# Seven block products for half of B's query and key projections, with B's V of those tokens moved ahead of the rest

## The chip, the cores and the metric

One core of a Trainium2 chip runs the whole program. The metric is the device time of one execution in microseconds; the kernel before takes 1763.98 us (median of 3 runs, 1763.06 to 1763.99).

The core has a matrix engine (TensorE, PE in the profile, with its weight loads as PEld), a vector engine (DVE), a scalar engine (ACT), a general engine (POOL, GpSimd) and a queue that starts transfers (SP). Matmul results stand in eight banks of PSUM, each 128 rows of 512 numbers.

## The reference

Two attention blocks on 2048 tokens of 640 numbers, each with 32 heads of 20, and their results side by side:

```python
qkv = x @ wqkv                        # A and B: 2048 x 1920
# A: each query sees 8 keys, at distances 0, 2, ..., 14 behind it
logits = einsum("bhsd,bhswd->bhsw", q, kg) * Dh ** -0.5     # masked, softmax over 8
# B: full attention
scores = einsum("bhqd,bhkd->bhqk", q, k) * Dh ** -0.5       # softmax over 2048 keys
out = concatenate([A(o) @ wo, B(o) @ wo], axis=-1)
```

## The kernel before, in words

Every product of two fp32 matrices is made of three matmul passes: each operand is cast to a rounded high part on ACT, the low part (value minus high part) is made by a subtract on DVE, and PE adds high x high, high x low and low x high (PASSES, line 30: pairs of weight part and x part). A projection of one tile therefore takes 5 row parts of 128 (KC) x 3 passes = 15 matmuls.

The program is written out in one order. `pe`, `act`, `dve`, `gp` and `sp` (class InOrder, line 49) pin each instruction behind the one written before it on the same engine, so an engine never passes a waiting instruction; between engines only data and buffers order the work. Since all of them record through line 61, the profile shows this line for everything, and one reads it by tiles. `after(n, fn)` (line 80) puts work off to the n-th `tick()` from now; the main loops call `tick` once per group of matmuls, so work put off lands at a fixed group.

The stages, in the order of PE's queue:

1. A's projections (lines 524 to 578): four weight column groups n, twelve token tiles t of 128 each, 15 matmuls per tile, each result copied by ACT (`a_store`) and stored to DRAM. The other four token tiles of A are done later, in the loop. At tile 5 of each group `a_keep` copies the split weights to DRAM (`wa_d`, eight transfers) for them. During the last group B's inputs are loaded and split (`x_pieces`, `m_pieces`: DMA to a staging tile, cast on ACT, subtract on DVE).
2. B's q and k (lines 615 to 655): five pairs of weight blocks m (128 columns each, order MS: the five blocks of k, then of q) x four token blocks n of 512 x two blocks j, 40 groups of 15 matmuls of 128x512. The result is cast by ACT (`pr`), its low part made by DVE from PSUM, and both are stored to DRAM (`qb_d`, `kb_d`). Banks come from a rotation over all eight. The next pair's weights are loaded at n = 1 and split two ticks later.
3. B's V (lines 1026 to 1063): 30 groups (`v_group`) of 15 matmuls of 128x320, for token blocks 2, 3, 0, 1 and two halves of the columns; the last two groups (LAG) run inside the loop. ACT copies each into one of four tiles `ve` whose extra columns of ones were set at the start by POOL (`ones`). From the seventh group on each is followed by one step of maxima, `b_max`: four matmuls of q against k in two pairs of banks (`wide()`, two such pairs, banks 4 to 7) and two reduces on DVE, which give the running maximum of each query row; 24 steps (LEAD) are needed before the loop. Since x tiles 0 and 1 gave their place to q and k of attention, they are loaded and split a second time (groups 8 and 16).
4. The loop (from line 1094): scores, exponentials, the product with V and the rest of the maxima in a written order (UNIT, UNIT_V, ...), with A's remaining work between, and at the end both output projections.

A's own attention is POOL's work: `a_attention` (line 450) is a generator of pieces, each a handful of elementwise instructions on tile `akv`, whose data was fetched by SP two pieces before. `next(a_work)` writes one piece; twelve are written among the 40 groups of q and k and eight among the V groups. B's keys and queries for the loop (tiles `bk`, `bq`) are loaded by `b_keys` and `b_queries` in the last q and k groups and the first V groups.

Of the kernel before, what the change touches and what calls it, by code (L numbers as in the profile page):

```python
# [21 lines left out]
KC = 5  # L22
# [16 lines left out]
PB = 6  # L39
# [26 lines left out]
def attention_pair(ctx, tc, xa, wqk_a, wv_a, wo_a, xb, wqk_b, wv_b, wo_b, oa, ob):  # L66
# [270 lines left out]
    ones = [sb.tile([128, 16 * VC + 11], F32, tag=tag, bufs=2, name="ve") for tag in ("raw", "rb", "raw", "rb")]  # L337
    for t in ones:
        gp.memset(t, 1.0)
# [182 lines left out]
    MS = [5, 6, 7, 8, 9, 0, 1, 2, 3, 4]  # L522
    XB, WB = [], []
# [17 lines left out]
    for n in range(NA):  # L541
        nxt = None
        for t in range(UP):
# [20 lines left out]
            if n == 1 and t == 7:  # L564
                w, more = x_pieces(xb, 0)
                XB.append(w)
                loads += more
            if n == NA - 1:
                if t in (1, 2):
                    w, more = m_pieces(MS[t - 1])  # L570
                    WB.append(w)
                    more[0]()
                if t % 4 == 0 and t:
                    w, more = x_pieces(xb, t // 4)
                    XB.append(w)
                if t > 4 and t % 4:
                    more.pop(0)()
        W = nxt
    wait[0] = 2
    w, loads = x_pieces(xb, 3)  # L580
    XB.append(w)
# [34 lines left out]
    for m in range(0, 10, 2):  # L616
        nxt = []
        for n in range(4):
            for j in range(2):
                p = next(banks)  # L620
                for k in range(KC):
                    for i, (wi, xi) in enumerate(PASSES):
                        pe.matmul(p, WB[j][:, wi, k], chunk(XB[n], xi, k), start=(k == 0 and i == 0),
                                  stop=(k == KC - 1 and i == 2))
                c = MS[m + j]
                o = (0, 1) if c < KC else (1, 0)
                pt = sb.tile([128, 2, 512], F32R, tag="p", bufs=PB, name="pr")
                act.copy(pt[:, o[0]], p)
                dve.tensor_tensor(pt[:, o[1]], p, pt[:, o[0]].bitcast(F32), ALU.subtract)
                after(1, sp.dma_start, dst_b(c, n).rearrange("t p c -> p t c"), pt.bitcast(F32))  # L630
                tick()
                if loads:
                    loads.pop(0)()
                if m < 8 and (n, j) in ((1, 0), (1, 1)):
                    w, loads = m_pieces(MS[m + 2 + len(nxt)])
                    nxt.append(w)
                elif m == 8 and (n, j) == (0, 1):
                    WV, loads = wide_pieces(wv_b[0])
                elif m == 8 and n == 3:
                    if j == 0:  # L640
                        wait[0] = 4
                        w1, more = wide_pieces(wv_b[1])
                        for fn in more:
                            fn()
                if m == 8 and n > 1:
                    if (n, j) == (2, 0):
                        k_loads = b_keys(0)
                        rings.append(big(1, [128, NQC, 2, 512], "bq"))
                        q_loads = [fn for qc in range(NQC) for fn in b_queries(0, qc)]
                    k_loads.pop(0)()  # L650
                groups += 1
                if 4 < groups < 34 and groups * 2 % 5 < 2:
                    next(a_work, None)
        WB = nxt
    tick()

    def max_rows(m4, m1, q, qc):

        mt = sb.tile([128, 3, 32], F32R, tag="mtr", bufs=2, name="mtr")
# [366 lines left out]
    for n, half, s in V_GROUPS[:-LAG]:  # L1028
# [6 lines left out]
        if groups == 1:  # L1035
            wait[0] = 5
# [155 lines left out]
```

## Time and profile before

| | |
|---|---|
| time, median of 3 runs | 1763.98 us (1763.06 to 1763.99) |
| profiled execution: span from the first to the last instruction | 1761.2 us |
| granted clock of TensorE, mean | 1.000 |
| A's projections | 0 to 161.6 us |
| B's q and k | 161.6 to 300.5 us |
| B's V with 24 steps of maxima | 300.5 to 389.4 us |
| the loop and the end | 389.4 to 1761.2 us |
| busy: PE, DVE, ACT, POOL | 1749.3, 1345.8, 1333.5, 1229.1 us |

The profiled execution has no time of its own beside its span; the median lies 2.8 us above that span, and that difference (start and end of the execution around the first and the last instruction) is taken as the same for both kernels. A row of the timeline reads: start, duration, engine, line, operation, tile written <- tile read, shapes, count, and in brackets the idle time before it with what ended it. A row of the stretches reads: from:to, length, busy time of PE, weight loads, DVE, ACT and POOL with instruction counts, granted clock, share of the DMA engines, GB/s. PE's busy time holds the modelled ends of pipelined matmuls, so the distance between starts is what a matmul costs.

### The profile page before, as it was taken

How to read it: one execution, taken by the hardware profiler on the slowest of the kernel's cores; microseconds unless marked ns; L12 is line 12 of the kernel's file. 1: busy time of each engine (PE TensorE's matmuls, PEld its weight loads, DVE VectorE, ACT ScalarE, POOL GpSimd, SP SyncE). 2: the span in 40 equal slices, each digit the busy share in tenths (PEclk: the TensorE clock that was granted, in tenths of full speed). 3: DMA queues.
4: the chain of work that ended last, by engine and by line, in shares of the span. 5: the costliest groups of instructions: out<-in, count | busy, mean ns of one | idle time of the engine just before them, and what ended most of it. 6: DMA issues, size and time to landing. Idle time of an engine off the chain costs nothing.

```text
span 1761.2 us, 31938 instructions
## 1 busy us (share of the span) xinstructions
PE 1749.3 (99%) x11331; PEld 997.6 (57%) x11331; DVE 1345.8 (76%) x1821; ACT 1333.5 (76%) x2598; POOL 1229.1 (70%) x1086
## 2 busy tenths in 40 slices
PE   9999999999999999999999999999999999999999
PEld 8988888874444444444444444444444444444569
DVE  3102333679999999999999999999999999999400
ACT  4323222229989999999999999999999999989881
POOL 0000683595888888888989898988888898745442
PEclk9999999999999999999999999999999999999999
DMA  7657867774536554644474456536552634222223
GB/s 261 196 170 246 303 236 265 240 234 118 160 98 172 145 161 127 160 131 133 157 178 129 135 150 156 161 103 172 148 154 91 158 100 138 62 73 63 60 71 112
DMA packets 215176, 269.74 MB, mean 153 GB/s; under 512 B 91724, under 2 KB 131788, under 8 KB 215016
## 3 DMA queue, kind: packets, MB, share of 16 engines
q1 hardware_dynamic: 214440, 267.04, 51.3%
q8 instruction: 89, 1.46, 0.4%
q14 instruction: 71, 0.58, 0.1%
q10 hardware_dynamic: 576, 0.66, 0.1%
HBM read 192.87 MB, written 74.74 MB: 152 GB/s over the span
## 4 chain that ended last, share of the span: by engine, by line
PE 95%; DVE 2%; ACT 1%; DMA 1%; issue 1%; POOL 0%; SPq 0%; DVEq 0%; POOLq 0%; ACTq 0%
PE ps_st L61 95%; DVE mx L61 1%; ACT e L61 1%; DMA bq<-qb_d 1%; DMA stg<-wv_b 0%; ACT more L61 0%; DVE mtr L61 0%; SPq L61 0%; POOL am L61 0%; ACT al L61 0%; ACT pr L61 0%; DVE ww L61 0%; POOL ident L61 0%; ACT ro L61 0%; DVE am L61 0%
## 5 line engine op out<-in xcount | busy, mean ns | idle before, releaser
L61 DVE TENSOR_REDUCE mx<-ps_st 128x1 f32<-128x512 f32 (+1 forms) x1500 | 1217.4, 877 | 75.5 <-PE ps_st L61 64.7
L61 ACT ACTIVATE e<-ps_st 128x512 f32<-128x512 f32 x2048 | 1067.4, 609 | 34.2 <-PE ps_st L61 14.3
L61 PE MATMUL ps_st<-bq,bk 62*128 62x512 f32 x2048 | 611.4, 439 | 0.2
L61 PEld LDWEIGHTS ps_st<-bq,bk 62*128 62x128 f32 x2048 | 287.8, 184 | 479.2 <-ACT e L61 336.8
L61 PE MATMUL ps_st<-bk,bq 60*128 60x512 f32 x2048 | 556.2, 434 | 1.9 <-DVE mx L61 0.9
L61 PE MATMUL ps_st<-e,vb 128*32 128x512 f32 x4096 | 542.9, 604 | 2.2
L61 POOL TENSOR_TENSOR braw<-braw,more 128x512 f32<-128x512 f32 x224 | 288.1, 1286 | 140.4 <-ACT more L61 136.7
L61 POOL TENSOR_TENSOR akv<-akv,aq 128x1280 f32<-128x1280 f32 x64 | 188.5, 2945 | 184.5 <-DMA akv<-ka_d 184.5
L61 POOL TENSOR_TENSOR akv<-akv 128x640 f32<-128x640 f32 (+3 forms) x304 | 282.8, 930 | 23.8
L61 PEld LDWEIGHTS ps_st<-bk,bq 60*128 60x128 f32 x2048 | 265.3, 184 | 34.6 <-DVE mx L61 12.2
L61 ACT COPY ro<-ps_st 128x320 f32<-128x320 f32 (+2 forms) x132 | 62.5, 475 | 191.1 <-PE ps_st L61 158.8
L61 PEld LDWEIGHTS ps_st<-e,vb 128*32 128x32 f32 x4096 | 82.0, 108 | 156.2 <-issue 70.6
L61 POOL TENSOR_TENSOR akv<-akv,al 128x1280 f32<-128x1280 f32 x64 | 152.0, 2375 | 0.2
L61 ACT COPY more<-ps_st 128x512 f32<-128x512 f32 x224 | 132.4, 591 | 2.1 <-PE ps_st L61 1.4
L61 PE MATMUL ps_st<-ww,xn 128*128 128x320 f32 x768 | 126.0, 314 | 0.5 <-ACT e L61 0.5
L61 PEld LDWEIGHTS ps_st<-ww,xn 128*128 128x128 f32 x768 | 113.6, 188 | 20.8 <-ACT e L61 8.8
L61 PE MATMUL ps_st<-xn,w 128*128 128x512 f32 x480 | 117.6, 393 | 0.0
L61 PEld LDWEIGHTS ps_st<-xn,w 128*128 128x128 f32 x480 | 90.1, 188 | 21.0
L61 ACT CAST pr<-ps_st 128x512 fp32r<-128x512 f32 x40 | 23.5, 587 | 103.6 <-PE ps_st L61 103.6
L61 PE MATMUL ps_st<-wc,xn 128*128 128x512 f32 (+1 forms) x432 | 101.2, 379 | 0.0
L61 DVE TENSOR_TENSOR pr<-ps_st,pr 128x512 fp32r<-128x512 f32 x40 | 27.6, 691 | 92.4 <-ACT pr L61 89.6
L61 PEld LDWEIGHTS ps_st<-wc,xn 128*128 128x128 f32 x432 | 80.1, 189 | 13.7
(71 smaller groups left out, 1066.6 us busy)
## 6 DMA issues: line engine op xcount, KB each, us to landing
akv<-ka_d SPq DMA_DIRECT2D x128, 320.0 KB
akv<-va_d SPq DMA_DIRECT2D x128, 320.0 KB
wx<-wa_d SPq DMA_DIRECT2D x24, 480.0 KB
kb_d<-pr SPq DMA_DIRECT2D x20, 512.0 KB
qb_d<-pr SPq DMA_DIRECT2D x20, 512.0 KB
bk<-kb_d SPq DMA_DIRECT2D x16, 640.0 KB
bq<-qb_d SPq DMA_DIRECT2D x64, 160.0 KB
rb<-s_d SPq DMA_DIRECT2D x128, 64.0 KB
```

The source lines that it names most:

```text
L61: return self.tc.keep_in_program_order(op(*a, **k))
```

## The change

Tokens 0 to 1023 (two token blocks) and a pair of weight blocks form a two by two product. Over the first four of the five row parts, taken as two halves of two parts each, it is made by seven block products and sums of operands and results in place of eight block products (the scheme of Strassen in Winograd's form); the fifth row part is added in the plain way. `XPair` loads the two token blocks, makes the split tiles that are used as they are (`base`), the sums (`turns`, four adds or subtracts on DVE for each half) and their split tiles `T` (`second`). `WPair` does the same for a pair of weight blocks: `x` (and `y`, `z`) are the split tiles of the blocks and of their sums. `b_quad` writes the products in eight runs of matmuls, of 6, 6, 9, 6, 6, 9, 9 and 3, over five banks, with the sums of results on DVE, and yields four times, once for each finished result. Low parts of the results are put off through `lows`.

The order of the stages becomes: A's projections; five pairs on tokens 0 to 1023 (four steps each); 16 V groups of tokens 0 to 1023; q and k of tokens 1024 to 2047 (20 groups of 15 matmuls as before, weights loaded and split again); 14 V groups of tokens 1024 to 2047. The second load of x tiles 0 and 1 is gone. The four memsets of `ones` stand behind the pairs. The 24 steps of maxima: one behind each of the last four q and k groups, then two behind each odd and one behind each even V group. B's keys for the loop are loaded at q and k groups 13 to 16, its queries from group 14 on. A's 20 pieces: six in the pairs, four in the first V groups, seven in q and k, three in the last V groups. Some tiles change places (`last0`/`last1`, homes 0 and 2).

The core of the diff:

```diff
-    MS = [5, 6, 7, 8, 9, 0, 1, 2, 3, 4]
+    MS = ((5, 6), (7, 8), (9, 0), (1, 2), (3, 4))
+    class XPair:
+        def load(self, i):
+            t = sb.tile([128, 1024], F32, tag="p", bufs=PB, name="stg").rearrange("p (k c) -> p k c", c=512)
...
+        def base(self, j):
+            u = columns(self.n + j)
+            XB[self.n + j] = u
+            for kp in range(2):
+                self.parts(u[0], 2 * kp, self.raw[kp, j])
+            self.parts(u[1], 0, self.raw[2][:, j:j + 1])
+        def parts(self, u, k, raw):
+            m = raw.shape[1]
+            act.copy(u[:, 0, k:k + m], raw)
+            dve.tensor_tensor(u[:, 1, k:k + m], raw, u[:, 0, k:k + m].bitcast(F32), ALU.subtract)
+        def sums(self, kp):
+            a, b = self.raw[kp, 0], self.raw[kp, 1]
+            turns(dve, a, b, lambda t, k: t[:, k])
+        def second(self, j):
+            self.T[j] = u = big(self.homes[j], [128, 2, KC - 1, 512], "xs")
+            for kp in range(2):
+                self.parts(u, 2 * kp, self.raw[kp, j])
...
+    class WPair:
...
+        def base(self):
+            a, b = self.raw
+            self.parts(self.x, 0, a)
+            self.parts(self.y, KC - 1, b[:, 1:KC - 1:2])
+            self.parts(self.x, KC, b[:, KC - 1:])
+        def sums(self):
+            a, b = self.raw
+            at = lambda t, k: t[:, k:KC - 1:2]
+            dve.tensor_tensor(at(b, 1), at(b, 0), at(b, 1), ALU.add)
+            dve.tensor_tensor(at(b, 0), at(a, 0), at(b, 0), ALU.subtract)
+            dve.tensor_tensor(at(a, 0), at(b, 1), at(a, 0), ALU.subtract)
+            dve.tensor_tensor(at(a, 1), at(a, 1), at(a, 0), ALU.subtract)
+            self.parts(self.z, 0, a[:, :KC - 1])
+            self.parts(self.y, 0, b[:, :KC - 1])
...
+    def b_parts(p, c, n, first=None, late=True):
+        o = (0, 1) if c < KC else (1, 0)
+        pt = sb.tile([128, 2, 512], F32R, tag="p", bufs=PB, name="pr")
+        src = p
+        if first is not None:
+            src = pt[:, o[1]].bitcast(F32)
+            dve.tensor_tensor(src, first, p, ALU.add)
+        act.copy(pt[:, o[0]], src)
+        def lo():
+            dve.tensor_tensor(pt[:, o[1]], src, pt[:, o[0]].bitcast(F32), ALU.subtract)
+            b_store(pt, c, n)
...
+    def b_quad(w, x):
...
+        product(b[0], of(w.x, 0), of(X1, 0), True, True)
+        act.copy(c[0], b[0])
+        product(b[1], of(w.z, 0), of(x.T[0], 0), True, True)
+        dve.tensor_tensor(c[1], c[0], b[1], ALU.add)
+        low()
+        product(b[0], of(w.x, 1) + v1, of(X1, 1) + l1, False, True)
+        b_parts(b[0], m[0], n)
+        yield
+        product(b[1], of(w.y, 0), of(x.T[1], 1), False, True)
+        low()
+        product(b[2], of(w.y, 1), of(x.T[1], 0), True, True)
+        dve.tensor_tensor(c[0], c[0], b[1], ALU.add)
+        dve.tensor_tensor(c[1], c[1], b[2], ALU.add)
+        product(b[3], of(w.z, 1) + v1, of(X2, 1) + l2, True, True)
+        b_parts(b[3], m[0], n + 1, c[1])
+        yield
+        product(b[4], A22 + v2, of(x.T[0], 1) + l1, True, True)
+        b_parts(b[4], m[1], n, c[0])
+        low(1)
+        yield
+        product(b[2], v2, l2, False, True)
+        b_parts(b[2], m[1], n + 1, c[0])
+        low(1)
+        yield
...
+                if t == 0:
+                    x_pair = XPair(0, (2, 3))
+                if t < 5:
+                    x_pair.load(t)
+                if t == 5:
+                    x_pair.base(0)
+                elif t == 7:
+                    x_pair.base(1)
+                elif t == 6:
+                    pairs_w = [WPair(*MS[0])]
+                elif t == 8:
+                    x_pair.sums(0)
+                    x_pair.sums(1)
+                elif t == 9:
+                    pairs_w[0].base()
+                    pairs_w[0].sums()
+                elif t == 10:
+                    x_pair.second(0)
         W = nxt
+    x_pair.second(1)
...
+    for m in range(5):
+        w = pairs_w.pop()
+        for n, _ in enumerate(b_quad(w, x_pair)):
+            tick()
+            groups += 1
+            piece(5, 8, 10, 13, 15, 18)
+            if m < 4:
+                if n == 0:
+                    pairs_w = [WPair(*MS[m + 1])]
+                elif n == 2:
+                    pairs_w[0].base()
+                elif n == 3:
+                    pairs_w[0].sums()
+            elif n == 0:
+                WV, more = wide_pieces(wv_b[0])
+                for fn in more:
+                    fn()
+    low()
...
-    V_GROUPS = [(n, half, s) for n in (2, 3, 0, 1) for half in range(2) for s in range(4 * n, 4 * n + 4)]
...
+    for groups in range(1, 17):
+        half, s = divmod(groups - 1, 8)
...
+        v_group(s // 4, half, s)
+        tick()
...
+    for m in range(5):
+        nxt = []
+        for n in (2, 3):
+            for j in range(2):
+                p = bank()
+                product(p, [lambda i, k=k: WB[j][:, i, k] for k in range(KC)],
+                        [lambda i, k=k: chunk(XB[n], i, k) for k in range(KC)], True, True)
+                give(p)
+                b_parts(p, MS[m][j], n, None, False)
+                tick()
...
+                if groups > 12 and k_loads:
+                    k_loads.pop(0)()
...
+                if groups > 16:
+                    for i in islice(steps, 1):
+                        b_max(i)
+        WB = nxt
+    v_late = [(3, 1, 14), (3, 1, 15)]
+    for groups in range(1, 15):
...
+        v_group(2 + s // 4, half, 8 + s)
+        tick()
...
+        for i in islice(steps, 1 + (groups % 2)):
+            b_max(i)
```

225 lines of the change are left out of this document (132 added, 93 removed).

## The prediction

> **What bounds the kernel now.** I read the page first, then the stretch table by stage, then the timelines of TensorE, the other engines and the DMA queue around the changed stages, and the groups of instructions for durations.
>
> ```profile
> span 1761.2 us, 31938 instructions
> PE 1749.3 (99%) x11331; PEld 997.6 (57%) x11331; DVE 1345.8 (76%) x1821; ACT 1333.5 (76%) x2598; POOL 1229.1 (70%) x1086
> PE 95%; DVE 2%; ACT 1%; DMA 1%; issue 1%; POOL 0%; SPq 0%; DVEq 0%; POOLq 0%; ACTq 0%
> ```
>
> TensorE (PE) is busy 99% of the span, and the chain that ended last is 95% PE. The sum is therefore a sum over PE's queue: matmuls that go, and time in which PE stands still.
>
> ```profile
> 0.00:161.60 161.60, 160.24 (x739) 137.32 (x740) 30.77 (x43) 52.70 (x91) 3.43 (x14) 1.00 0.67 215
> 161.60:300.50 138.90, 138.90 (x602) 112.63 (x601) 46.91 (x59) 35.24 (x58) 85.58 (x74) 1.00 0.77 265
> 300.50:389.40 88.90, 87.34 (x548) 73.34 (x546) 60.78 (x62) 20.15 (x41) 57.98 (x48) 1.00 0.81 249
> ```
>
> The rows are A's projections, B's q and k, and B's V with the first maxima; the columns after the stretch are PE, weight load, DVE, ACT and POOL, granted clock, DMA share, GB/s. In q and k PE never stops, while DVE works 47 us and ACT 35 of 139: there each has all the slack it could want. The change spends that slack, and the question is whether it spends it at times when PE isn't waiting.
>
> **What goes.**
>
> ```profile
> 161.62 2.96 PE L61 MATMUL ps_st<-xn,w 128*128 128x512 f32 x12
> 164.42 0.86 PE L61 MATMUL ps_st<-xl,w 128*128 128x512 f32 x3
> 165.11 2.95 PE L61 MATMUL ps_st<-xn,w 128*128 128x512 f32 x12
> ```
>
> One group of 15 matmuls takes 165.11 - 161.62 = 3.49 us, so 0.233 each. A pair of weight blocks against two token blocks takes 4 x 15 = 60 matmuls now; the generator b_quad issues 6+6+9+6+6+9+9+3 = 54. Five pairs save 30 matmuls: 30 x 0.233 = 7.0 us. The second half (tokens 1024 to 2047) keeps its 300 matmuls, V its 32 groups.
>
> **What is added: the handover between pairs.** Every engine takes its instructions in the order of the code. The casts and subtracts that prepare the next pair (base) are issued after the product b[4] has been added up on DVE, and the sums after b[2]; behind b[4] only three matmuls of the old pair are left on PE. So PE must stand while ACT and DVE work through that list.
>
> ```profile
> 182.59 0.59 ACT L61 CAST pr<-ps_st 128x512 fp32r<-128x512 f32 x1 [2.39 <-PE ps_st L61]
> 183.07 0.73 ACT L61 CAST w<-stg 128x640 fp32r<-128x640 f32 x1
> 183.21 0.69 DVE L61 TENSOR_TENSOR pr<-ps_st,pr 128x512 fp32r<-128x512 f32 x1 [2.21 <-ACT pr L61]
> 183.84 0.83 DVE L61 TENSOR_TENSOR w<-stg,w 128x640 fp32r<-128x640 f32 x1
> ```
> ```profile
> L61 DVE TENSOR_TENSOR wd<-stg,wd 128x256 fp32r<-128x256 f32 x7 | 2.9, 419 | 3.9 <-ACT wd L61 3.9
> L61 ACT CAST wd<-stg 128x256 fp32r<-128x256 f32 x7 | 2.8, 407 | 0.0
> L61 PEld LDWEIGHTS ps_st<-xn,w 128*128 128x128 f32 x480 | 90.1, 188 | 21.0
> L61 ACT CAST xn<-stg 128x1024 fp32r<-128x1024 f32 x16 | 16.6, 1050 | 8.1 <-DMA stg<-xa 4.2 <-DMA stg<-xb 3.9
> ```
>
> A 512-wide cast takes 0.59 and lets the next start after 0.48; DVE's 512-wide step is 0.69, the next after 0.61 to 0.63; 640 wide 0.73 and 0.83; 256 wide 0.41 and 0.42. The other engine starts 0.03 after the one it waits for (182.59 + 0.59 to 183.21). Zero is the end of b[4]. DVE adds it until 0.72; ACT casts the result until 1.34 and the 640 columns of w.x from 1.23 to 1.96; DVE has subtracted b[3]'s low part by then and makes w.x's low part until 2.8. The 256 and 128 columns take it to 3.3, the add of b[2] to 4.0, b[4]'s low part to 4.6, the four sums (256 wide, 0.34 apart) to 6.0. ACT casts w.z until 6.6, DVE subtracts until 7.3.
>
> PE is through with b[2] at 0.53. Its next product needs w.x, its weight: high part at 1.96 plus a weight load of 0.19, low part from the third matmul on at 3.0; it ends at 3.93 instead of 0.53 + 1.40 = 1.93, 2.0 late. The second product needs w.z: high at 6.75, low at 7.5, end 8.4 instead of 3.93 + 1.40, 3.1 late. A handover costs 5.1 us, four of them 20.4. The cast of c[0] and the add c[1] fit inside the following nine matmuls.
>
> The first pair: ACT and DVE do both base calls, the eight adds of x_pair.sums and the weights' preparation during A's last five groups. From the store copy of group 7 (161.62 - 4 x 3.49 = 147.7) three casts and three subtracts bring DVE to 152.3, eight adds to 157.2, weights and their sums to 159.9, ACT's two casts of them to 160.9. Behind these stand group 10's copy, two 1024-wide casts (1.05 each) and group 11's copy, ending at 163.8. That copy empties bank 0, in which the first product starts: 164.0 instead of 161.62, 2.4 late. T[1] then lands while nine matmuls run.
>
> ```profile
> 148.00 1.24 SPq L61 DMA_DIRECT2D stg<-xb  x1
> 154.73 1.05 ACT L61 CAST xn<-stg 128x1024 fp32r<-128x1024 f32 x1 [2.73 <-DMA stg<-xb]
> ```
>
> The loads for this don't set it: x_pair's five are issued ahead of the weights' copy to wa_d in the SP queue, and the pair's two weight blocks take the place of this load, which came right behind that copy and was there 6.7 us after its issue: about 155 to 156, when ACT gets to them. If they came 2 us later, so would PE's start.
>
> ```profile
> 302.68 1.92 PE L61 MATMUL ps_st<-ww,xn 128*128 128x320 f32 x12
> 304.88 1.92 PE L61 MATMUL ps_st<-ww,xn 128*128 128x320 f32 x12
> ```
> ```profile
> L61 POOL MEMSET ve<- 128x347 f32 x4 | 1.4, 388 | 0.0
> ```
>
> V's start: a group is 2.20 us, 0.147 a matmul. Its weight parts are issued at the last pair's third step, behind the same b[4] chain: cast at 1.96, low part at 2.8, so that the third matmul starts at 3.0 and the group ends at 4.9 instead of 0.53 + 2.20: 2.2 late. The four memsets of ones move behind the pairs in POOL's queue; ACT's copies wait for them, but PE has four banks, 8.8 us, before that reaches it, so I put 1.4 us of memsets at nothing.
>
> **POOL beside it.** Six pieces of A's attention now run beside the pairs.
>
> ```profile
> 188.57 2.97 POOL L61 TENSOR_TENSOR akv<-akv,aq 128x1280 f32<-128x1280 f32 x1 [184.47 <-DMA akv<-ka_d]
> 195.43 2.96 POOL L61 TENSOR_TENSOR akv<-akv,aq 128x1280 f32<-128x1280 f32 x1
> 239.10 2.96 POOL L61 TENSOR_TENSOR akv<-akv,aq 128x1280 f32<-128x1280 f32 x1
> ```
> ```profile
> 239.38 3.37 DVE L61 TENSOR_TENSOR w<-stg,w 128x640 fp32r<-128x640 f32 x1
> 242.67 0.68 DVE L61 TENSOR_TENSOR pr<-ps_st,pr 128x512 fp32r<-128x512 f32 x1
> ```
> ```profile
> L61 DVE TENSOR_TENSOR w<-stg,w 128x640 fp32r<-128x640 f32 x7 | 10.3, 1472 | 0.0
> ```
>
> The subtract of 0.83 took 3.37 when it met POOL's 2.96: it ends 0.69 behind POOL's end at 242.06. The one that reads PSUM (pr) is as short as ever. The seven w subtracts from 185 to 300 us average 1.472, 0.64 above the undisturbed. [...] In the handover ten steps of DVE read two SBUF tiles (two low parts, three of base, four sums, w.z): at 0.64 each 6.4, four times 25.6. POOL has six pieces of 195.43 - 188.57 = 6.86, 41 us, of a stage of 62.8 + 25 + about 5, so 44%: 11.3. Three of the ten wait for ACT anyway: 8 us. Bounds 0 (it finds POOL idle each time) and 25.6.
>
> **The second half.** Its q and k are 20 groups as before; m_pieces, stores and pieces keep their old distances, and the extra weight reloads (each 0.35 to 0.5 us of queue) lie a group ahead of their use, so I put them at nothing; a late one would show as a PE wait of up to 2 us. The reload of B's tokens 0 to 1023 goes, off the path. The first maxima come four groups before the end of q and k, right behind the loads of k (groups 13 to 16) and q.
>
> ```profile
> 304.52 3.48 SPq L61 DMA_DIRECT2D bq<-qb_d  x4
> 316.30 0.47 PE L61 MATMUL ps_st<-bk,bq 60*128 60x512 f32 x1 [0.26 <-DMA bq<-qb_d]
> 317.18 0.71 PE L61 MATMUL ps_st<-bk,bq 60*128 60x512 f32 x3 [0.41 <-DMA bq<-qb_d]
> ```
>
> Here loads issued until 308.0 still held PE at 317.18, 9.2 later. The fourth k load is issued about 1.7 after group 16 (cast, subtract, store issue) and wanted one group, 3.49, after it: 1.7 + 9.2 - 3.5 = 7.4 late at most, 0 if it lands in 1.8. I take 4, the middle; 0.7 of waits here goes.
>
> Then 20 maxima stand in 13 V groups, two behind each odd group, where each used to have one.
>
> ```profile
> 326.33 0.73 PE L61 MATMUL ps_st<-bk,bq 60*128 60x512 f32 x4
> 326.88 2.36 DVE L61 TENSOR_REDUCE mx<-ps_st 128x2 f32<-128x1024 f32 x2 [0.71 <-PE ps_st L61]
> 326.99 2.03 PE L61 MATMUL ps_st<-ww,xn 128*128 128x320 f32 x12
> 368.22 2.34 DVE L61 TENSOR_REDUCE mx<-ps_st 128x2 f32<-128x1024 f32 x2
> 370.62 0.50 PE L61 MATMUL ps_st<-bk,bq 60*128 60x512 f32 x2 [0.63 <-DVE mx L61]
> 371.04 2.03 PE L61 MATMUL ps_st<-ww,xn 128*128 128x320 f32 x12
> ```
>
> One step is four matmuls, 326.99 - 326.33 = 0.66 us of PE, into the only two pairs of banks, and 2.36 of DVE, from 0.55 after the first. A second step behind it finds both pairs full: the last is free at 0.55 + 2.36 = 2.91, PE starts 0.06 after (370.56 to 370.62), and V goes on 0.42 later: 3.39 instead of 1.32. That is 2.07 each at seven odd groups, 14.5 us. The even groups give DVE time to catch up, no more.
>
> **The sum:** -7.0 - 0.7 + 2.4 + 20.4 + 2.2 + 8 + 4 + 14.5 = +43.8. On the profiled execution that is 1761.2 + 43.8 = 1805.0; the median of the runs, 1763.98, stands 2.8 above the span, so 1807.8. The loop behind keeps its written order, and nothing in it can catch up: PE is busy 99% there too. POOL enters it with as many pieces done as before.
>
> **Rivals.** (a) Only the pairs cost: the k loads land in time and PE's doubled maxima find banks free, 43.8 - 18.5 = +25.3, 1789.3. For it: DVE works 61 of 89 us in V. Against it: the wait of 0.63 with a reduce before it. 0.10. (b) The clock falls. In all three stage rows it is 1.00, but PE never stood for more than 0.63 in the rows shown, and it will for 3.1. If half clock holds for 3.49 us behind each of four handovers, half a group each is lost, 4 x 1.75 = 7: 1814.8. [...] 0.08. (c) Faster: ACT and DVE are through with the next pair's w.x and w.z when PE asks, and with the reduces as well, as in the stage rows of before, where no wait of PE on them shows: -7.7, 1756.3. It decides at base's first cast: instead of at 1.23 it would have to start 5.1 us sooner, before b[4] is done, and it is issued behind b[4]'s add. 0.05. Costs that just cancel the 7.7: 0.02. The forecast itself 0.75.
>
> **Numbers.** Low end: no port waits, loads in time, half of the maxima's cost: 2.4 + 20.4 + 2.2 + 7.2 - 7.7 = +24.5, 1788; I go to 1786 for case (a). High end: the forecast with 18 for the port and 7.4 for the loads, +57, 1821, and with part of (b) 1826. A difference under 0.2% (3.5 us) is about what a measurement of this kernel can't tell from none. Faster 0.05, same 0.02, slower 0.93.
>
> **What would show it.** PE's q/k part for tokens 0 to 1023 is 270 matmuls of 62.8 us but takes some 90; in each handover two gaps of 2 and 3 us, the first ended by w, the second by w.z or their DVE steps; at odd V groups a gap of 2 us ended by mx; a DMA wait at the first maxima. Wrong if PE stays over 95% busy from 161 to 230 us, or if w.x's casts run before b[4]'s add.

## The result, and the profile after

The changed kernel takes 1855.17 us (median of 4 runs, 1853.71 to 1857.71), the kernel before 1763.92 us (4 runs, 1763.06 to 1763.99): ratio 1.052, 95% interval 1.0505 to 1.0535. It is 91 us slower. The forecast was 1807.8 us, so the sign was right and the size half of what it should have been; 1855 lies 29 us above the top of the range.

The page of the changed kernel, its span, its busy time by engine, and the chain that ended last:

```profile
span 1853.6 us, 32023 instructions
PE 1774.8 (96%) x11301; PEld 1011.1 (55%) x11301; DVE 1422.0 (77%) x1914; ACT 1349.8 (73%) x2632; POOL 1223.7 (66%) x1080
PE 78%; DVE 4%; ACT 1%; DMA 1%; issue 1%; POOL 0%; SPq 0%; DVEq 0%; ACTq 0%
```

PE executes 30 matmuls fewer (11301 against 11331) and is still busy 25 us longer (1774.8 against 1749.3). A busy time that grows while the count falls means slower matmuls, not only waits. The stretch table of the changed kernel says where: A, the pairs, the first 16 V groups, the second half's q and k, the last 14 V groups, the loop. The last three columns are granted clock, DMA share, GB/s.

```profile
0.00:161.98 161.98, 160.10 (x739) 136.56 (x739) 37.02 (x56) 52.51 (x93) 2.11 (x10) 1.00 0.65 210
161.98:274.65 112.67, 76.58 (x271) 56.59 (x271) 70.69 (x91) 29.41 (x54) 43.91 (x41) 0.85 0.48 167
274.65:310.50 35.85, 35.54 (x240) 35.29 (x241) 16.31 (x17) 15.06 (x29) 24.01 (x22) 1.00 0.82 287
310.50:405.34 94.84, 76.45 (x318) 58.48 (x316) 39.48 (x47) 19.95 (x34) 55.86 (x43) 0.92 0.78 245
405.34:482.70 77.36, 63.76 (x292) 50.31 (x291) 52.83 (x50) 7.16 (x16) 25.20 (x23) 0.79 0.42 126
482.70:1853.60 1370.90, 1362.33 (x9448) 673.85 (x9446) 1205.67 (x1656) 1225.68 (x2409) 1072.64 (x942) 1.00 0.46 128
```

A and the loop are as long as before (161.6 and 1371.8 there). Everything lies between 162 and 483 us: 320.7 us where the kernel before took 227.8. By the forecast's own terms they should have taken 131.0 for pairs and first V groups (62.8 + 2.4 + 20.4 + 8 + 2.2 + 16 x 2.20), 76.4 for q and k (20 x 3.49 + 4 x 0.66 + 4) and 61.9 for the last V groups: 14 groups with a step of maxima each at 329.39 - 326.33 = 3.06, as in the kernel before (its row is below), and seven more steps at 0.66 + 2.07. They took 148.5, 94.8 and 77.4, together 51 more.

```profile
329.39 0.74 PE L61 MATMUL ps_st<-bk,bq 60*128 60x512 f32 x4
```

The granted clock is 0.85, 0.92 and 0.79 in the three stages that contain long waits, and 1.00 in the first 16 V groups, where the longest is 0.31.

TensorE's timeline of the changed kernel, the rows at the starts of the first three pairs and of V:

```profile
165.46 2.93 PE L61 MATMUL ps_st<-xn,w 128*128 128x512 f32 x6 [3.31 <-ACT ro L61]
180.94 2.81 PE L61 MATMUL ps_st<-xn,w 128*128 128x512 f32 x6 [1.43 <-ACT w L61]
185.90 2.93 PE L61 MATMUL ps_st<-xs,w 128*128 128x512 f32 x6 [2.15 <-ACT w L61]
188.63 1.64 PE L61 MATMUL ps_st<-xn,w 128*128 128x512 f32 x6
202.78 3.02 PE L61 MATMUL ps_st<-xn,w 128*128 128x512 f32 x6 [4.20 <-ACT w L61]
212.68 1.22 PE L61 MATMUL ps_st<-xs,w 128*128 128x512 f32 x2 [6.88 <-ACT w L61]
274.65 0.55 PE L61 MATMUL ps_st<-ww,xn 128*128 128x320 f32 x2 [1.42 <-ACT ww L61]
```

Two stands in each handover, both ended by `w`, as forecast, and one at V's start. But look at the durations too: six matmuls behind a stand take 2.81 to 3.02 us, the same six at 188.63 take 1.64. They run at half speed, wholly or for the most part. The granted clock shows it directly. Read in stretches of a quarter microsecond, it is 1.00 or 0.50 and between them only where it changes, here at 164.90, 168.31, 181.97, 188.79 and 202.45 us: the distances are 1, 4, 2 and 4 times 3.41. Cut at such places, the changed kernel's stretches around the first handover are:

```profile
178.56:181.97 3.41, 1.85 (x8) 0.91 (x7) 2.34 (x4) 1.75 (x4) 0.00 (x0) 1.00 0.26 100
181.97:185.38 3.41, 1.78 (x4) 0.86 (x4) 3.12 (x8) 0.77 (x2) 0.00 (x0) 0.50 0.43 162
185.38:188.79 3.41, 2.89 (x7) 2.27 (x8) 1.29 (x2) 1.47 (x3) 0.00 (x0) 0.50 0.12 46
188.79:192.20 3.41, 3.41 (x17) 2.74 (x16) 1.81 (x3) 0.59 (x1) 0.00 (x0) 1.00 0.31 116
```

The first of them holds the stand of 1.43, and the two behind it run at 0.50. The second handover's stands, 4.20 and 6.88, are much longer than the first's; DVE's and POOL's timelines of the changed kernel show why (the sums and low parts for the second pair, then for the third, and what POOL did then):

```profile
183.40 1.80 DVE L61 TENSOR_TENSOR stg<-stg 128x256 f32<-128x256 f32 x4
185.88 1.29 DVE L61 TENSOR_TENSOR w<-stg,w 128x512 fp32r<-128x512 f32 x2 [0.68 <-ACT w L61]
208.18 3.80 DVE L61 TENSOR_TENSOR stg<-stg 128x256 f32<-128x256 f32 x4
212.66 4.85 DVE L61 TENSOR_TENSOR w<-stg,w 128x512 fp32r<-128x512 f32 x2 [0.68 <-ACT w L61]
```
```profile
204.81 2.90 POOL L61 TENSOR_TENSOR akv<-akv,aq 128x1280 f32<-128x1280 f32 x1
207.78 3.91 POOL L61 TENSOR_TENSOR akv<-akv 128x640 f32<-128x640 f32 x4
212.11 2.90 POOL L61 TENSOR_TENSOR akv<-akv,aq 128x1280 f32<-128x1280 f32 x1
```

The same four sums take 1.80 us with POOL idle and 3.80 beside its instructions, the two low parts 1.29 and 4.85. In the second half the first maxima wait for their keys, and a chain leads back to the transfer (timeline, then the chain of waits in this stretch):

```profile
375.39 0.47 PE L61 MATMUL ps_st<-bk,bq 60*128 60x512 f32 x1 [4.17 <-DMA bq<-qb_d]
386.62 1.19 PE L61 MATMUL ps_st<-bk,bq 60*128 60x512 f32 x3 [10.76 <-DMA stg<-wv_b]
387.73 4.17 PE L61 MATMUL ps_st<-xn,w 128*128 128x512 f32 x12
422.12 0.49 PE L61 MATMUL ps_st<-bk,bq 60*128 60x512 f32 x2 [1.09 <-DVE mx L61]
423.25 0.50 PE L61 MATMUL ps_st<-bk,bq 60*128 60x512 f32 x2 [0.64 <-DVE mx L61]
```
```profile
362.10 6.78 DMA qb_d<-pr
368.90 13.06 DMA bk<-kb_d
382.44 4.09 DMA stg<-wv_b
```

4.17 + 10.76 = 14.9 us of PE standing. These matmuls read no `wv_b`: the timeline names the transfer that landed at that moment, and the chain goes back through it to a k load that took 13.06 us from issue to landing. The fourth k load, issued at 374.27, is needed as well; it took 12.3 us at most. The last two rows are an odd V group: 1.09 + 0.64 = 1.73 of stands ended by `mx`.

### The profile page after: what moved, and what is told of

Same layout as the page of the kernel before. It is cut to its first block, busy times and chain, and to the rows that moved or that the text cites. A ratio compares the mean times of both kernels' runs of the same rounds, so it can differ in the third digit from the quotient of the medians.

```text
span 1853.6 us, 32023 instructions
## 1 busy us (share of the span) xinstructions
PE 1774.8 (96%) x11301; PEld 1011.1 (55%) x11301; DVE 1422.0 (77%) x1914; ACT 1349.8 (73%) x2632; POOL 1223.7 (66%) x1080
## 4 chain that ended last, share of the span: by engine, by line
PE 78%; DVE 4%; ACT 1%; DMA 1%; issue 1%; POOL 0%; SPq 0%; DVEq 0%; ACTq 0%
PE ps_st L61 78%; DVE mx L61 3%; ACT e L61 1%; DMA bk<-kb_d 1%; DMA qb_d<-pr 0%; DVE ww L61 0%; DVE w L61 0%; DMA stg<-wv_b 0%; ACT more L61 0%; POOL am L61 0%; ACT ww L61 0%; ACT w L61 0%; ACT pr L61 0%; ACT al L61 0%; DVE mtr L61 0%
## 5 line engine op out<-in xcount | busy, mean ns | idle before, releaser
L61 POOL TENSOR_TENSOR akv<-akv 128x640 f32<-128x640 f32 (+3 forms) x304 | 287.1, 944 | 23.8
L61 PE MATMUL ps_st<-ww,xn 128*128 128x320 f32 x768 | 135.6, 330 | 2.2 <-ACT ww L61 1.4
L61 PEld LDWEIGHTS ps_st<-ww,xn 128*128 128x128 f32 x768 | 123.2, 202 | 19.0 <-ACT e L61 8.7
L61 PE MATMUL ps_st<-xn,w 128*128 128x512 f32 x330 | 91.2, 422 | 13.4 <-ACT w L61 8.5
L61 PEld LDWEIGHTS ps_st<-xn,w 128*128 128x128 f32 x330 | 65.9, 204 | 34.4 <-ACT w L61 10.2
L61 ACT COPY ve<-ps_st 128x320 f32<-128x320 f32 x32 | 13.7, 427 | 96.2 <-PE ps_st L61 71.4
L61 ACT CAST pr<-ps_st 128x512 fp32r<-128x512 f32 x25 | 14.7, 588 | 92.7 <-PE ps_st L61 76.3
```

The costliest lines, as they stand in the source:

```text
L61: return self.tc.keep_in_program_order(op(*a, **k))
```

## The experiments

The theory after the result: the stands are where the forecast put them, but each also takes TensorE's clock to half for some microseconds, and the k loads take longer than supposed. Rivals: the summed products cost only by DVE's steps that last longer beside POOL; the second half's order is harmless; the k loads are late because other transfers crowd them. The kernel before took 1763.7, 1764.9, 1763.1 and 1763.4 us on the chips of the four sets of runs. The changed kernel's four executions span 4 us, so where a kernel ran once, a difference of that size in the total says nothing; stretches and stands are read within one trace each.

**Order without sums.** Eight plain products for tokens 0 to 1023, everything else as changed.

```diff
-        for n, _ in enumerate(b_quad(w, x_pair)):
+        for n, j in ((0, 0), (0, 1), (1, 0), (1, 1)):
+            product(p, [lambda i, k=k: WB[j][:, i, k] for k in range(KC)],
+                    [lambda i, k=k: chunk(XB[n], i, k) for k in range(KC)], True, True)
```

> The changed order of the stages with eight plain block products (300 matmuls, groups of 15) for tokens 0 to 1023: no sums, no seven products. By the theory this stage runs without a gap as before (70 us), V follows at once, and all that is lost behind it stays: 16 us at the first maxima and some 30 in q and k's end and the last V groups, about 1811, 47 above the kernel before. By the rival that the seven products are the whole loss: 1765.

Measured 1818.9 us in one execution. The order alone costs 55 us and the seven products another 36: a little more than the theory's 1811, and far from the rival's 1765. The stage without gaps that was expected did not come: some 8 of the 55 lie ahead of the second half's q and k (a stand of 3.32 for weights with half speed behind it, and V's start). The other 47 lie behind: the first maxima wait 4.44 + 10.49 for keys, and the odd V groups have the same stands of 1.10 + 0.64.

**POOL away from the pairs.** The six pieces beside the pairs move behind them, to see what POOL costs there.

```diff
-            piece(5, 8, 10, 13, 15, 18)
+            piece(20)
...
-        piece(3, 7, 11, 15)
+        piece(2, 5, 8, 11, 14)
...
-                piece(2, 5, 8, 11, 14, 17, 19)
+                piece(1, 3, 5, 7, 9, 11, 13, 15, 17, 18, 19)
```

> The changed kernel with five of the six pieces of A's attention moved from beside the pairs into the V groups and q and k groups behind them. [...] If POOL is innocent and the chain of DVE and ACT is long by itself: 1855 as before, handover gaps of 4 to 7 us remain.

Measured 1858.87 us in one execution: no gain in the total. The stretch of the pairs of this kernel and, of its timeline, one handover:

```profile
165.35:262.90 97.55, 78.29 (x271) 58.57 (x271) 51.23 (x87) 25.73 (x48) 0.00 (x0) 0.85 0.36 130
```
```profile
201.84 2.05 PE L61 MATMUL ps_st<-xn,w 128*128 128x512 f32 x6 [1.42 <-ACT w L61]
206.80 2.93 PE L61 MATMUL ps_st<-xs,w 128*128 128x512 f32 x6 [2.90 <-ACT w L61]
209.52 2.76 PE L61 MATMUL ps_st<-xn,w 128*128 128x512 f32 x6
280.59 3.57 PE L61 MATMUL ps_st<-ww,xn 128*128 128x320 f32 x12 [8.07 <-ACT ve L61]
```

The pairs took 97.55 instead of 109.19 (165.46 to 274.65), so taking POOL away was worth 11.6 us. Every handover now has the same two stands, 1.42 and 2.90. The gain went at once: the memsets of ones stood behind the moved piece on POOL, ACT's copies behind them, and PE waited 8.07; later weights came 3.05 late and the keys 15.5. So the total is that of an innocent POOL, but its stands of 4 to 7 us in the handovers did not stay. The pairs are still 97.55 for 270 matmuls of 62.8: 4 x 4.32 of stands and 1.42 at V make 18.7, and 16.0 are left, with a clock of 0.85. PE's busy time multiplied by (1 - granted clock), half a microsecond at a time, accounts for 13.3 of them; the rest stays unexplained.

**Something for PE to do in the stands.** On top of that, 12 and 9 useless matmuls in each pair, in the places of the two stands.

```diff
+        def filler(p, count):
+            for _ in range(count):
+                pe.matmul(p, w.x[:, 0, 0], X1[:, 0, 0], start=True, stop=True)
...
+        filler(b[2], 12)
...
+        filler(psb[:, (turn_of[0] + 2) % 8], 9)
```

> e1 with useless matmuls in the two gaps of each handover: 9 behind the last product of a pair, 12 between the first and the second product, 4.9 us of PE work per pair. If the granted clock falls because PE stands, and the matmuls behind a gap run at half speed, the clock of this stage stays at 1.00 and the kernel gains 1 to 3 us per pair on e1 although it does 4.9 us more work in each: about 1828. If the clock is not tied to the gaps, nothing is won: e1's time or up to 3 us more.

Measured 1858.6 us in one execution. The stretch of the pairs of this kernel and the same handover in its timeline:

```profile
165.07:255.99 90.92, 90.46 (x375) 70.83 (x376) 51.74 (x87) 26.28 (x49) 0.00 (x0) 0.98 0.40 141
```
```profile
199.91 6.44 PE L61 MATMUL ps_st<-xn,w 128*128 128x512 f32 x27
206.45 1.93 PE L61 MATMUL ps_st<-xs,w 128*128 128x512 f32 x6
208.22 1.55 PE L61 MATMUL ps_st<-xn,w 128*128 128x512 f32 x6
```

With 105 matmuls more the stretch is 6.6 us shorter, the clock 0.98 instead of 0.85, and the matmuls behind the place of the stand take 1.93 and 1.55 instead of 2.93 and 2.76. Nothing but the idle time was taken away, so the half speed comes from it. The earlier V start was again given back, to weights 3.79 late and to keys 18.3 late, and the expected total missed.

**The next pair prepared a pair earlier.** Weights are loaded a pair ahead, `base` and `sums` stand at the first and second step.

```diff
+    pairs_w.append(WPair(*MS[1]))
...
-                    pairs_w = [WPair(*MS[m + 1])]
-                elif n == 2:
                     pairs_w[0].base()
-                elif n == 3:
+                elif n == 1:
                     pairs_w[0].sums()
+                elif n == 3 and m < 3:
+                    pairs_w.append(WPair(*MS[m + 2]))
```

> The changed kernel with the next pair's weights loaded one pair earlier, its casts and subtracts issued at a pair's first step and its sums at the second, V's weight parts at the last pair's second step. By the theory (the order puts the preparation behind b[4]) the gaps between pairs go: pairs of 12.6 to 14 us, the stage 70 instead of 112.7, about 1815. By the rival that DVE has too much work beside POOL: pairs stay at 17 or more, 1835.

Measured 1841.26 us in one execution, 14 less than changed, a third of the gain of 40 that was expected. The stands move: 1.4 to 5.0 us each, five of eight ended by `sum`, above all the copy of c[0], which stands on ACT behind the casts of the sums that DVE makes under POOL: so it seems from the order of the code. To tell that from DVE's and ACT's own work, the same with the pieces moved as above:

> Seven products, the next pair prepared a pair early (as in the run with early preparation) and no piece of A's attention beside the pairs (five in V's first part, eleven in q and k instead). Theory (what still held PE with early preparation was DVE's sums under POOL, which hold ACT's queue): from first product to V's start 97.8 us falls to 70 to 75, with one or two waits under 2 us a pair. Rival (ACT and DVE's own work in a pair is too long): 85 or more, waits of 3 to 5 us stay. The total is about 1845 in either case, since the pieces' work comes back in the stages behind, as it did without early preparation.

Measured 1843.03 us (1841.03 to 1843.96; ratio 1.0446, 1.043 to 1.0462). The stretch of the pairs with early preparation and, below it, with early preparation and without the pieces:

```profile
165.66:263.43 97.77, 75.98 (x271) 57.15 (x272) 67.20 (x85) 26.03 (x48) 44.72 (x41) 0.84 0.53 185
```
```profile
165.36:244.37 79.01, 70.44 (x270) 54.53 (x271) 49.18 (x85) 26.24 (x48) 0.00 (x0) 0.92 0.47 160
```

79.0 instead of 97.8: between the 70 to 75 of the theory and the rival's 85, with one stand a pair left, of 1.89 to 2.38, ended by `sum` on ACT. Even so 270 matmuls take longer than the 300 of eight plain products would at full speed (69.8). The 18.8 us came back behind, 9.08 of them once more at `ve`.

**Keys and queries earlier.** All four k loads at groups 12 and 13, where the last block of k has just been stored, and the q loads at 2 to 9.

```diff
-                if groups > 12 and k_loads:
-                    k_loads.pop(0)()
-                if groups > 13 and len(q_loads) > 8:
-                    for fn in q_loads[:2]:
-                        q_loads.pop(0)()
+                if groups in (12, 13):
+                    for _ in range(2):
+                        k_loads.pop(0)()
+                if 1 < groups < 10:
+                    q_loads.pop(0)()
```

> The changed kernel with B's keys loaded at q and k groups 12 and 13 (two a group) and the first eight query loads at groups 2 to 9, instead of keys at 13 to 16 and queries at 14 to 17. If the wait of 4.2 + 10.8 us at the first maxima is the landing of loads issued too late into a full queue, it goes, and with it the half clock behind it: 15 to 17 us less, about 1839. If the DMA engines are simply full there, the wait stays: 1850 or more.

Measured 1845.28 us in one execution, 9.9 less than changed where 15 to 17 were expected. The wait for keys is 1.16 instead of 14.9; 1.66 and 1.87 for weights come in, whose load, issued behind the k loads, took 14.41 us.

**Useless matmuls between the doubled maxima**, on top of the early loads: seven ahead of the second step's first pair of banks, four ahead of its other. DVE's work is the same.

```diff
+            if fillers:
+                t = bank()
+                for _ in range(fillers - 3 * j):
+                    pe.matmul(t[:, :320], chunk(XB[3], 0, 0)[:, :128], WV[0][0][:, 0], start=True, stop=True)
+                give(t)
...
+            b_max(i, 7 if i != two_steps[0] else 0)
```

> e5 with useless matmuls between the two steps of a doubled pair of maxima in the last V groups: 7 in front of the second step's first pair of banks and 4 in front of its second, 1.6 us of PE work in gaps of 1.1 and 0.6. The gaps themselves stay as DVE sets them. If the slow V groups behind them (3.5 to 4.4 us instead of 2.2) are the clock's answer to the gaps, they return to about 2.2 and the kernel gains 10 to 13 us on e5, about 1828. If gaps are all there is, it gains nothing, 1839 or up to 3 more.

Measured 1835.18 us in one execution, 10.1 less than without them. Not all of that is theirs: the stretch in which they stand begins 4.5 us earlier, and up to there the two programs are the same. That stretch, the last V groups up to the loop's first score, with early loads alone and then with the fill:

```profile
397.62:474.80 77.18, 63.44 (x307) 50.36 (x305) 52.76 (x50) 7.58 (x17) 25.17 (x23) 0.83 0.43 128
```
```profile
393.12:463.90 70.78, 66.62 (x384) 52.21 (x383) 54.14 (x50) 7.57 (x17) 23.00 (x21) 0.98 0.49 141
```

77 matmuls more, 6.4 us less, clock 0.98 instead of 0.83. The prediction's way of counting (stands of 1.7 us and full speed between) would have made the fill free at best.

**Maxima one at a time**, on top of the early loads: from group 15 on, some in the middle of a product, and none doubled.

```diff
+                if groups + 1 in (16, 18, 19, 20):
+                    product(p, ws[:3], xs[:3], True, True)
+                    b_max(next(steps))
+                    product(p, ws[3:], xs[3:], False, True)
...
-                if groups > 16:
+                if groups > 14:
...
-        for i in islice(steps, 1 + (groups % 2)):
+        for i in islice(steps, 1):
```

> e5 with one step of maxima behind each of q and k groups 15 to 20, one more in the middle of groups 16, 18, 19 and 20, and one behind each of the last 14 V groups: never two in a row. If doubled steps wait for banks and then lose clock, the last V groups take 3.1 us each as in the kernel before, 44 instead of 77 us, at 5 us more in q and k: about 28 less than e5, 1811. If the V groups are slow for another reason (x or weights late): 1835.

Measured 1832.94 us in one execution, 12.3 less. The V groups run almost free of stands, but the first maxima, two groups sooner, wait 1.70 + 8.74 for keys. The total is near the rival's 1835, but not for its reason, since the V groups are not slow any more; the theory's 1811 missed.

**What makes the keys late.** First, four of A's pieces moved from the second half's q and k to the V groups, so that their loads don't share the DMA engines with the k loads:

```diff
-                piece(2, 5, 8, 11, 14, 17, 19)
+                piece(2, 5, 8)
...
-        piece(2, 5, 8)
+        piece(1, 3, 5, 7, 9, 11, 13)
```

> The changed kernel with four pieces of A's attention (groups 11, 14, 17, 19 of q and k for tokens 1024 to 2047) moved to the V groups behind, so that their loads of keys and values don't share the DMA engines with the k loads. Theory (the k loads are late because the DMA engines are full): the waits of 4.2 and 10.8 at the first maxima fall to 6 to 9 together, the k loads land 8 to 10 us after issue, total about 1849. Rival (a k load takes 12 to 14 us by its own form, or is issued late): the waits stay at 14 to 15, total 1853 to 1856.

Measured 1849.89 us (1848.6 to 1852.98; ratio 1.0489, 1.0472 to 1.0507). The waits are 3.07 + 10.76 = 13.8. The total is 5.3 less, as the theory of crowding had it, but only 1.1 of that is in these waits: A's loads are not what makes the keys late. The stores of q (512 KB each) and the weights' loads, which stand beside the k loads too, were not taken away. Then the k loads themselves, at half the bytes (the keys of tokens 1024 to 2047 of the first group of heads are left out):

```diff
-            k[r * HALF + r0:r * HALF + r0 + n].bitcast(F32),
-            kb_d[:, s0:s0 + n, g * GH + 2 * r:g * GH + 2 * r + 2].rearrange("c p h n -> p c h n"))
+            k[r * HALF + r0:r * HALF + r0 + n, :c].bitcast(F32),
+            kb_d[:c, s0:s0 + n, g * GH + 2 * r:g * GH + 2 * r + 2].rearrange("c p h n -> p c h n"))
```

> The changed kernel with the first four k loads cut to half their bytes: they bring the keys of tokens 0 to 1023 only, and zeros stand for the other keys of this group of heads (that part of the computation is left out). Same issue times, same row length. Theory (the 13 to 15 us from issue to landing is the transfer of the k loads themselves, 2 MB in rows of 2 KB into 22 and 40 partitions): the waits of 4.2 and 10.8 at the first maxima fall together to 5 to 8. Rival (it is the stores of the summed products that stand ahead of them and beside them, or SP that issues the loads late): 13 to 15 stay.

Measured 1848.59 us (1846.48 to 1850.69; ratio 1.0483, 1.0453 to 1.0514). The row of PE's first long wait and the chain of waits of this kernel:

```profile
378.24 1.19 PE L61 MATMUL ps_st<-bk,bq 60*128 60x512 f32 x3 [6.70 <-DMA bk<-kb_d]
```
```profile
364.30 5.25 DMA bk<-kb_d
369.57 8.54 DMA bk<-kb_d
```

6.70 instead of 14.9. The last k load is issued at 369.57 instead of 374.27, and lands after 8.54 instead of 12.3. Part of why the issue was late is in SP's waits in the changed kernel from 355 to 392 us (total, times, longest):

```profile
SPq L61 <- DMA bk<-kb_d: 8.8, 3, 5.2
```

Of these 8.8, 3.6 (2.0 and 1.6) lie ahead of the fourth k load's issue, where the kernel with half the bytes has 0.2; the 5.2 lies behind it. So 8.2 of the 14.9 us hang on the k loads' own bytes: by their transfer, and by the delay that they give each other's issue. What makes up the other 6.7 is not shown.

**All of it together**: early preparation, A's last copies and the front's preparation a few tiles sooner, early loads, single maxima from group 15 (the edits above, and these):

```diff
-            if t == 5:
+            if t == (5 if n < NA - 1 else 8):
                 a_keep(n, W)
...
-                elif t == 8:
+                elif t == 6:
+                    x_pair.base(1)
                     x_pair.sums(0)
                     x_pair.sums(1)
-                elif t == 9:
+                elif t == 8:
                     pairs_w[0].base()
                     pairs_w[0].sums()
```

> Seven products with the preparation early (as e3), the first pair's inputs prepared one to two groups sooner with the copy of A's weights behind them, loads early (e5) and single maxima (e6). By the theory PE's queue has no gap left but small ones: 7.0 us of matmuls less than the kernel before, the loop starting at about 385 us instead of 389, 1758 to 1764. [...]

Measured 1819.0 us (1817.04 to 1820.97; ratio 1.0304, 1.026 to 1.0348): 36 less than changed, but far from the kernel before, and above the expected 1758 to 1764. The front's stand falls from 3.31 to 0.72; the pairs keep eight stands of 1.8 to 5.0 us, seven of them ended by ACT, and the keys are waited for 2.14 + 8.39. With maxima from group 17 instead, doubled three times, and four pieces behind the k loads:

```diff
-                if groups + 1 in (16, 18, 19, 20):
+                if groups + 1 > 17:
...
-                if groups > 14:
+                if groups > 16:
...
-        for i in islice(steps, 1):
+        for i in islice(steps, 1 + (groups in (5, 9, 13))):
...
-                piece(2, 5, 8, 11, 14, 17, 19)
+                piece(2, 5, 8)
```

> Everything together: early preparation, earlier front, early k loads, maxima from group 17 and doubled only three times, four pieces of A's attention moved behind the k loads. Theory: against the earlier combined version at 1819.0 the wait of 10.5 for k at groups 15 and 16 goes with the half clock behind it: 1800 to 1806. Rival (the maxima then crowd DVE at the end): 1815 to 1820. Neither beats the kernel before.

Measured 1820.68 us (1815.97 to 1822.22; ratio 1.0317, 1.0297 to 1.0337). The keys are there, and the maxima crowd instead: stands for `mx` of 2.55 + 0.63 and 1.38 + 0.34 at a doubling in the last V groups. The total is the rival's.

**Order alone, mended**: plain products, early loads, maxima from group 17, three doubled (the last two edits, on the plain products).

> Order alone (eight plain products, no summed blocks), with the k loads at groups 12 and 13, the q loads earlier, and the maxima spread: from group 17 on with one in the middle of a product, doubled only at V groups 5, 9 and 13. Theory (the order costs its 55 us by loads that land late, by PE's stands for the maxima's banks, and by the half clock behind these stands): first maxima wait of 15 falls to about 2, four of seven doublings go with their half clock, so 1818.9 - 13 - 20, about 1786, clock of the last V groups above 0.9. Rival (DVE can't do 24 maxima of 2.4 us in the time that is left, wherever they stand): the gaps move, total 1805 to 1815.

Measured 1801.37 us (1800.2 to 1804.75; ratio 1.0214, 1.0193 to 1.0235): 17.5 of the order's 55 us, between theory and rival. It is the best of the new order, without a single summed product, and still 38 us behind the kernel before. PE still stands 2.65 for `mx` in q and k, and 2.77, 2.25 and 1.09 at the three doublings: 24 steps have 4 q and k and 14 V groups to lie beside, where the kernel before gave one V group to each. Between A's projections and the loop this kernel's stands add up to 22.6 us: 12.5 for `mx`, 9.5 for weights (4.04 at one place in the first half) and 0.6 for keys. PE's busy time multiplied by (1 - granted clock) adds 12.9. That is nearly all of the 38. None of the kernels tried beats the one before.

## Why the prediction was wrong in size

**Right: the places of the stands.** The handover was put at 2.0 + 3.1; undisturbed it is 1.42 + 2.90, each ended by `w` as said. V's start 1.42 + 0.31 (2.2), first pair 3.31 (2.4), no cost of the memsets (true only as long as no piece stands ahead of them), the doubled maxima 1.73 of standing with a restart behind it (2.07), DVE's longer steps beside POOL 11.6 (8). Together these terms are 46.0 measured (seven doublings at 1.73) against 47.5 in the sum; that POOL's excess and the shorter handovers cancel in it is luck. The forecast's range speaks of a port here: no run shows one, only that DVE's steps last longer beside POOL (four sums 3.80 instead of 1.80 us, two low parts 4.85 instead of 1.29) and that the pairs without it take 11.6 us less. The answer to the first question, that the change spends DVE's and ACT's slack where PE waits for them, held.

**Wrong: the clock, rival (b).** The step that failed is that the sum takes the clock at 1.00 throughout and has no term for half speed. Rival (b) had it at a chance of 0.08 and 7 us, for half clock over 3.49 us behind each handover. Both were the author's guess: the kernel before, with a clock of 1.00 in all three stages, shows neither. A stand of 1.43 brought it, and with one of 2.15 it lasted (2.81 and 2.93 for six matmuls instead of about 1.5). Without POOL the pairs lose 13.3 us by it, 2.7 each. And rival (b) looked only at the handovers: the doubled maxima, stands of 1.09 + 0.64 every ten microseconds, take the last V groups to 0.79. There the stage is 15.4 over its forecast, and filling the stands made the stretch 6.4 shorter although it added work. Taken over half microseconds of the changed kernel's trace, PE's busy time multiplied by (1 - granted clock) adds up to 11.7 us in the pairs, 2.2 in the second half's q and k and 16.0 in the last V groups: 29.9 of the 51 us by which these stages exceed the forecast.

The length of a stand does not decide it alone. With early preparation TensorE's timeline has this row:

```profile
184.69 1.66 PE L61 MATMUL ps_st<-xn,w 128*128 128x512 f32 x6 [1.92 <-ACT sum L61]
```

A stand of 1.92 left the next six matmuls at full speed, and one of 1.43 in the changed kernel brought 2.81. The difference is where they fall among the stretches of 3.41 us at whose ends alone the clock changed: in the traces of all fourteen kernels of the new order, the 277 distances between one change and the next are whole multiples of 3.41, and so are the 30 of the changed kernel's trace by itself. The 1.43 (179.51 to 180.94) lies within one, and the 1.92 (182.77 to 184.69) across the end of one at 184.27. Cut that way between A's projections and the loop, the fourteen traces hold 959 stretches at full speed. The 75 in which PE was busy for less than 0.44 of the time were all followed by half speed, the 774 with 0.6 or more never; of the 110 between, 70 were. In the changed kernel's trace by itself (161.49 to 482.34 us) it is 70 stretches: 8 under 0.44, all followed by half speed, 51 of 0.6 or more, none, and 7 of the 11 between. So two short stands count together when they fall into one stretch, as 1.09 and 0.64 do: both lie between 420.90 and 424.31 us, where PE was busy 1.69 of 3.41 us, and the stretch behind ran at 0.50. No stretch has to be idle for it: in the one before 181.97 PE was busy 1.85 of 3.41 us.

**Wrong: the loads of k**, put at 4 with bounds 0 and 7.4. The bound took 9.2 us from issue to use from the loads of q in the kernel before. The k loads are 640 and 352 KB, those of q 160 and 80: the fourth was used 12.3 us after its issue, 3.1 more than the bound took (8.7 with half the bytes). And it was issued 3.1 us after PE was ready for it (374.27 against 371.2), where the forecast counted on 1.8 before: 4.8 more, in part SP's waits for earlier k loads. 14.9 instead of 4 is another 10.9. POOL's 3.6 over its term and the shorter stands of the handovers (17.3 instead of 20.4) about cancel.

**The other rivals.** (a), only the pairs cost, is far off: the order alone costs 55. (c), preparation ahead of PE, was not what the change does; made so, it took 79.0 us without POOL where 62.8 were wanted. The fall of -7.0 for 30 matmuls was real, and nothing of it could be seen.

What stays open: why the loops of the kernels with and without fill in the pairs differ by 3 us; what decides for the clock between 0.44 and 0.6 of busy time; and what makes the keys late beside their own bytes.

## What to carry to other kernels

Cutting matmuls pays only if what prepares them lies in time that TensorE does not wait for; seven products for eight save one part in ten here, and one short chain of casts and sums at each handover eats it several times over (1.42 + 2.90 us of stands without POOL, where a pair saves 1.4). Price each stand of TensorE with the half speed behind it, also for stands of one or two microseconds that recur: here each of the 75 stretches of 3.41 us with TensorE busy for less than 0.44 of it put at least the next 3.41 us at half speed, and in the changed kernel's last V groups 16.0 us of lost clock came on top of 13.6 us of such stands. A quick test is to fill them with useless matmuls and see whether the stage gets shorter. And when a stage is moved, list what it covered: V's groups were what DVE's maxima and the loads of k lay beside.

## What the runs showed that was not expected

The clock changed only at whole multiples of 3.41 us, so that of two stands the shorter could be the dearer one (1.43 against 1.92). Useless matmuls made a stage faster twice: 105 more in 6.6 us less, 77 more in 6.4 us less. A load issued behind the k loads took as long as they did (14.41 us for 320 KB of weights; 4.09 for such a load behind them once they had landed). And moving POOL's work out of one stage moved its whole cost into others, most of it by memsets that then stood behind a piece waiting for its data: 8.07 us.
